# A first stage of attention and MLP laid out as one list of pieces, with one unit's raw tensors kept in half of W2's place

## The chip, the cores and the metric

The kernel runs on one core of a Trainium2 chip. Its engines are PE (TensorE, matmuls), ACT (ScalarE), DVE (VectorE), POOL (GpSimd) and SP (SyncE, which here only issues DMAs). Each engine works through its own instructions in the order of the program and waits on semaphores for the others. The metric is the device time of one execution in microseconds (us); lower is better.

## The reference

Eight batches, twelve heads, 448 tokens, head width 64; then a layer norm and a two-layer MLP of width 768 and 3072 over the heads put side by side.

```python
q_n, k_n = (rmsnorm(q, g_q), rmsnorm(k, g_k))
scores = scale * np.matmul(q_n, k_n.transpose(0, 1, 3, 2))
attn = np.exp(scores - np.max(scores, axis=-1, keepdims=True))
attn = attn / (np.sum(attn, axis=-1, keepdims=True) + 1e-09)
x = np.matmul(attn, v)            # heads side by side: [B, S, 768]
xn = (x - mu) / np.sqrt(var + 1e-06) * g_ln
out = x + np.maximum(xn @ w_ch1, 0.0) @ w_ch2
```

## The kernel before

Heads are worked in pairs (six a batch, 48 in all), and pairs are loaded and normalised in units: units 0 to 3 are batch 0 (1, 1, 2 and 2 pairs), from unit 4 on every unit is two pairs, so units 4, 5 and 6 are batch 1, units 7, 8 and 9 batch 2. A unit's raw q, k and v lie in fp32 in a ring of two tiles (`p_in`, tag `qkv`). The first batch's raw v and q take these two tiles too, its keys lie in hT's place.

The preparation of a unit from 4 on is a dozen pieces named by a letter: b sets up, a squares the keys and c the queries (ACT), d and e sum the squares (DVE), g takes the root (ACT), i multiplies the keys by the gains (POOL), j rounds them to fp16 and k takes what is left over (DVE), l scales the queries and m doubles them, z copies the values (POOL). Then K and Q turn keys and queries on PE, C and D copy them out of PSUM (DVE). S is a score block on PE, E its exponential on ACT, V the product with the values on PE, O the evacuation with the division (DVE), T the statistics (DVE). In batch 0 the same letters serve with the pair or query part behind them (qa, qG, qt, qg, ql, qm, Q, QC are a query part's square, gain, sum, root, scale, doubling, turn and copy).

Batch 0 is treated apart: its three blocks of 128 queries (phases 0, 1, 2) are worked one behind the other, so that the MLP's first layer can begin on block t while the next block's attention runs. A, N and X are aggregation, norm and transpose of a block; U{t}.{k} is a sixth of the first layer for block t (24 matmuls of 128 columns), R{t}.{k} its relu. The second layer runs in four chunks of six matmuls for each block and half of the 768 columns.

The order up to the start of batch 1's attention is written out in `ORDER` and emitted for all five engines exactly so. It ends with the scores of pair 6 and the last block's norm; it holds U0.0 to U1.5, the preparation of unit 4 and the loads L4, L5 and L6. What follows comes from two merged lists: `mlp_chunks(0)` (U2.0 to U2.5, then the 24 down chunks, the left half of the columns first) and the attention steps (seven a pair), which `run_rest` lays between the chunks in proportion, leaving the last TAIL0 = 8 chunks behind the attention. `EARLY` places the pieces of units 5 to 9 among these steps, and a load of unit u + 2 follows unit u's pieces. Batch 1's norm follows the last attention step, its transposes are DMAs on SP's queue, and then batch 1's MLP begins (L878, psH). The later batches go the same way.

Queues: SP issues the loads of units up to 10 (each tensor is one main transfer and two small ones), gln, the DMA transposes and the stores; POOL issues the weights, W1 in three thirds (W0, W1, W2 in the list) and W2 in two halves by columns (W3, W4), at their place among its own instructions.

Some names and lines: U is L641 and R L646; S L585 (batch 0) and L333 (later), E L596 and L351, V L617 and L384 to L386; j and k of batch 0 L466 to L471; a and c L207, d and e L210, i L218, k L229, l L71, z L270 to L276; down chunk L894 and its sum L898; xnT's DMA L860; loads L125 and L133; W1 L785, W2 L790.

Of the kernel before, what the change touches and what calls it, by code (L numbers as in the profile page):

```python
# [27 lines left out]
POOL_HI, POOL_DUP = (0, 1, 2, 4, 5), (4,)  # L28
KN_POOL, COPY_ACT, DUP_POOL = (1,), ('C4', 'QC2.4'), ('2.0', '0.2')
# [3 lines left out]
spread a0 qa0.0 d0 a1 qG0.0 qt0.0 h0 d1 qg0.0 n0 h1 ql0.0 j0 qm0.0 n1 Q0.0 k0 QC0.0 K0 j1 C0  # L33
qa0.2 k1 S0.0.0 a2 S0.0.1 qG0.2 qt0.2 K1 C1 E0.0.0 G W0 d2 qg0.2 S0.1.0 a3 z0 ql0.2 h2 d3
E0.0.1 qm0.2 E0.1.0 S0.1.1 n2 z2 V0.0 Q0.2 h3 qa2.0 QC0.2 j2 n3 E0.1.1 W1 qa1.0 V0.1 k2 j3 z3
qt1.0 K2 C2 qg1.0 qG1.0 L4 k3 K3 S0.2.0 S0.2.1 E0.2.0 C3 E0.2.1 qG2.0 ql1.0 K4 V0.2 C4 S0.3.0
O0.0 S0.3.1 E0.3.1 K5 qm1.0 W2 T0.0 Q1.0 E0.3.0 C5 S0.4.0 G2 Q1.3 E0.4.0 QC1.0 S0.4.1 V0.3
E0.4.1 QC1.3 S0.5.0 E0.5.0 S0.5.1 qt2.0 V0.4 E0.5.1 S1.0.0 E1.0.0 V0.5 S1.0.1 O0.1 E1.0.1
S1.1.0 E1.1.0 S1.1.1 T0.1 V1.0 A0 E1.1.1 S1.2.0 N0 E1.2.0 S1.2.1 V1.1 X0 E1.2.1 S1.3.0 XC0
qg2.0 V1.2 S1.3.1 O1.0 E1.3.0 U0.0 E1.3.1 ql2.0 qa2.4 V1.3 T1.0 S1.4.0 qm2.0 R0.0 S1.4.1 qt2.4  # L40
U0.1 E1.4.1 qG2.4 qg2.4 Q2.0 E1.4.0 ql2.4 Q2.2 R0.1 V1.4 QC2.0 L5 S1.5.0 S1.5.1 QC2.2 E1.5.0
U0.2 qm2.4 E1.5.1 V1.5 R0.2 S2.0.0 O1.1 Q2.4 E2.0.0 S2.0.1 U0.3 T1.1 QC2.4 A1 N1 E2.0.1 S2.0.2
X1 R0.3 W3 S2.1.0 XC1 E2.1.0 U0.4 E2.0.2 S2.1.1 R0.4 U0.5 E2.1.1 S2.1.2 R0.5 S2.2.0 V2.0 E2.2.0
U1.0 b4 a4 E2.1.2 d4 i4 S2.2.1 U1.1 E2.2.1 R1.0 S2.2.2 R1.1 V2.1 W4 E2.2.2 S2.3.0 U1.2 c4 z4
# [31 lines left out]
class _Shared:  # L76
    pass


class _Fast:  # L80


    def __init__(self, ctx, tc, sh, q, k, v, gs, g_ln, w1, w2, out):
# [36 lines left out]
        self.late, self.preps, self.n_scores = [], {}, 0  # L120
# [62 lines left out]
    def pieces(self, u):  # L183
# [9 lines left out]
        def begin():  # L193
            c["t"] = self.loads.pop(u)
            c["ssq"] = self.p_n.tile([128, 2, 14], FP32, tag="ssq", name="ssq", bufs=4)[:, :, 0:g]
            c["rt"] = self.p_n.tile([128, 2, 14], FP32, tag="rt", name="rt", bufs=4)[:, :, 0:g]
            c["rb"] = self.p_n.tile([128, 2, 14], FP32, tag="rq", name="rr_all", bufs=6)[:, :, 0:g]
            c["r", 0], c["r", 1] = c["rb"][:, 0], c["rb"][:, 1]
            c["qn"] = self.p_n.tile([128, 14, 2, D], FP16, tag="qn", name="qn")[:, 0:g]
            c["khl"] = self.p_n.tile([128, 14, 2, D], FP16, tag="khl", name="khl")[:, 0:g]  # L200
            self.units[u] = (c["qn"], c["khl"], m, c["r", 1])

        def square(n):
# [3 lines left out]
            nc.scalar.activation(c["sq", n], c["t"][n], AFT.Square)  # L207
# [9 lines left out]
        def kg():  # L217
            nc.gpsimd.tensor_tensor(  # L218
                out=c["t"][1], in0=c["t"][1],
                in1=sh.gprod.unsqueeze(1).broadcast_to([128, g, D]), op=ALU.mult)  # L220

        def khi():
            if u in POOL_HI:
                nc.gpsimd.tensor_copy(out=c["khl"][:, :, 0], in_=c["t"][1])
            else:
                nc.scalar.activation(c["khl"][:, :, 0], c["t"][1], AFT.Identity)  # L226

        def klo():
            nc.vector.tensor_tensor(out=c["khl"][:, :, 1], in0=c["t"][1],  # L229
                                    in1=c["khl"][:, :, 0], op=ALU.subtract)  # L230

        def qn():
            if u < DMA_UNIT:
                _scaled(nc, c["qn"][:, :, 0], c["t"][0], c["r", 0])
                return
            x, r = c["t"][0], c["r", 0]
# [28 lines left out]
        def qdup():  # L265
            (nc.gpsimd if u in POOL_DUP else nc.vector).tensor_copy(out=c["qn"][:, :, 1],
                                                            in_=c["qn"][:, :, 0])

        def vmain():
            nc.gpsimd.tensor_copy(out=v16.rearrange("p s h j d -> p (s h) j d")[:, :, :, 0:D],  # L270
                                  in_=c["t"][2][:, 0:6 * m].rearrange("p (h j) d -> p h j d", j=3))

        def vleft():
            for e in range(2):
                r = slice(64 * e, 64 * e + 64)
                nc.gpsimd.tensor_copy(out=vl[r, :, e, 0:D], in_=c["t"][2][r, 6 * m:])  # L276
# [42 lines left out]
    def scores(self, p, i):  # L319

        nc = self.nc
        c = self.prs[p]
        u, w = PAIR_UNIT[p]
        both = u >= TWO_LEFT and i == 6
# [3 lines left out]
        if both and w:  # L328
            return
        ps = [self.score_bank(p + d) for d in range(2 if both else 1)]  # L330
        if i < 6:
# [13 lines left out]
        for d, x in enumerate(ps):  # L345
            if i < 6 or (p + d) % 2 == 0:
                o = c["E"][:, i]
            else:
                o = self.prs[p + d]["EL"] = self.p_e.tile([128, S], FP16, tag="EL", name="EL")
            g = self.group(p + d, i)  # L350
            nc.scalar.activation(out=o, in_=x[:, 0:S], func=AFT.Exp,  # L351
                                 scale=self.units[u][3][:, g:g + 1], bias=EXP_BIAS)

        if i == 6 and UNIT_PAIR[u] == p and u > 4:
# [13 lines left out]
    def values(self, p, i):  # L368
        nc = self.nc
# [17 lines left out]
        if i == 6:  # L387
            self.evac_o(p)
# [27 lines left out]
    def first_pieces(self):  # L416
# [34 lines left out]
        def key_unit(u, p0, m):  # L451
# [3 lines left out]
            def square():  # L455
                start(c, g, "khl")
                nc.scalar.activation(c["sq"], k, AFT.Square)

            def scale():
                eng = nc.gpsimd if u in KN_POOL else nc.vector  # L460
                eng.tensor_tensor(out=k, in0=k, in1=c["r"].unsqueeze(2).broadcast_to([128, g, D]),
                                  op=ALU.mult)

            def high():
                if u in POOL_HI:
                    nc.gpsimd.tensor_copy(out=c["n"][:, :, 0], in_=k)  # L466
                else:
                    nc.scalar.activation(c["n"][:, :, 0], k, AFT.Identity)
# [17 lines left out]
        def query_part(ph, p0, p1):  # L486
# [15 lines left out]
            def weight():  # L502
                for y in src:
                    nc.gpsimd.tensor_tensor(
# [11 lines left out]
            def double():  # L516
                eng = nc.gpsimd if tag in DUP_POOL else nc.vector
                eng.tensor_copy(out=c["n"][:, :, 1], in_=c["n"][:, :, 0])
# [33 lines left out]
        def values(z):  # L552
            p0, p1 = {0: (0, 2), 2: (2, 4), 3: (4, 6)}[z]
            nc.gpsimd.tensor_copy(
                out=self.v16[:, p0:p1, :, :, 0:D].rearrange("p s h j d -> p s (h j) d"),
                in_=tv[:, 6 * p0:6 * p1].rearrange("p (s g) d -> p s g d", g=6))
            for e in range(2):
                r = slice(64 * e, 64 * e + 64)
                nc.gpsimd.tensor_copy(out=self.vl[r, p0:p1, e, 0:D], in_=tv[r, 36 + p0:36 + p1])
# [85 lines left out]
        def relu(t, k):  # L645
            nc.scalar.activation(  # L646
                out=self.hT[:, 4 * k:4 * k + 4, ts(t, 128)],
                in_=o["up", t, k].rearrange("p (f s) -> p f s", f=4), func=AFT.Relu)
# [21 lines left out]
    def moved(self, name, out, ps):  # L670
        if name in COPY_ACT:
# [16 lines left out]
    def first_attention(self):  # L688
# [5 lines left out]
        ops = self.ops = self.first_pieces()  # L694
        for x in ORDER:
            key, n = x[0], x[1:]
            if x in ops:
                ops[x]()
            elif x == "batch1":
                self.batch(1)  # L700
            elif x == "spread":
                self.spread_g()
            elif key == "L":
                self.load_unit(int(n))
            elif x == "G":
# [481 lines left out]
```

## Time and profile before

| | us |
|---|---|
| three runs | 620.84, 623.96, 624.11; median 623.96 |
| the profiled execution | 621.17 |
| its span, first to last instruction | 619.5 |
| PE / DVE / ACT / POOL busy over the span | 580.2 / 296.5 / 356.5 / 190.6 |
| first matmul of batch 1's MLP | 139.36 |

A page of a profile shows one execution. Its rows of 40 digits are the busy share of each fortieth of the span in tenths; PEclk is the granted TensorE clock in the same way. Rows of windows give the busy time of each engine in a stretch, with the number of instructions, then the granted clock, the share of DMA time and the rate. Rows of groups name line, engine, operation, output and input, shapes and count, then busy time and the mean in ns of one, then the idle time ahead of them and what ended it. Rows of a timeline or of the chain give start and duration.

### The profile page before, as it was taken

The page shows a single profiled execution, that of the slowest core. Times are in us where ns is not written, and L with a number is a line of the kernel's source. Part 1 is how long each engine was busy: PE and PEld are TensorE (multiplying, and loading weights), DVE is VectorE, ACT ScalarE, POOL GpSimd, SP SyncE. Part 2 cuts the span into 40 slices and gives each one's busy share as a digit, 9 for nine tenths or more (in the row PEclk, how much of TensorE's full clock was granted, in tenths as well). Part 3 has the DMA queues.
Part 4 walks back from the last instruction along what each step waited for, and adds up shares of the span by engine and source line. Part 5 has one row for each costly group of instructions (what it writes and reads, how often), then busy time and mean ns, then how long its engine had stood idle before and what let it go on. Part 6 is the DMA issues. An engine that isn't in the chain of part 4 may idle for free.

```text
span 619.5 us, 12191 instructions
## 1 busy us (share of the span) xinstructions
PE 580.2 (94%) x4856; PEld 358.7 (58%) x4856; DVE 296.5 (48%) x634; ACT 356.5 (58%) x675; POOL 190.6 (31%) x250
## 2 busy tenths in 40 slices
PE   2499869979999999999999999999999999999997
PEld 1489756545456566655456566655556666654465
DVE  5974777772444535671453535662453531360011
ACT  4577767736875189726875189727875187214300
POOL 5843152233445055603535065503522000000000
PEclk9999989999999999999999999999999999999999
DMA  8999963358398468796367489666453420040011
GB/s 253 214 238 215 217 148 100 104 121 229 62 122 157 121 137 124 129 187 136 61 115 170 107 88 209 138 150 119 95 91 86 111 62 4 26 102 2 1 51 54
DMA packets 130224, 75.23 MB, mean 121 GB/s; under 512 B 96468, under 2 KB 120356, under 8 KB 130164
## 3 DMA queue, kind: packets, MB, share of 16 engines
q1 hardware_dynamic: 113092, 44.53, 36.9%
q0 software_dynamic: 16128, 29.27, 22.4%
q8 instruction: 39, 0.64, 0.4%
q10 hardware_dynamic: 944, 0.62, 0.4%
q14 instruction: 21, 0.17, 0.1%
HBM read 52.30 MB, written 11.01 MB: 102 GB/s over the span
## 4 chain that ended last, share of the span: by engine, by line
PE 83%; DVE 8%; ACT 2%; DMA 2%; issue 2%; POOL 1%; SPq 0%; DVEq 0%; ACTq 0%; POOLq 0%
PE psC L894 32%; PE psH L878 31%; PE psS L333 7%; PE oA L384 4%; PE psU L641 3%; PE oB L386 2%; PE psS L339 1%; DVE ssq L210 1%; ACT khl L207 1%; DMA xnT<-xn 1%; DVE xn L832 1%; DVE qn L71 1%; PE psS L585 1%; DVE khl L471 1%; DMA qkv<-in_v_dram 1%
## 5 line engine op out<-in xcount | busy, mean ns | idle before, releaser
L894 PE MATMUL psC<-w,hT 128*128 128x384 f16 (+1 forms) x1368 | 235.6, 323 | 0.0
L878 PE MATMUL psH<-xnT,w 128*128 128x512 f16 (+1 forms) x1008 | 218.4, 356 | 3.0 <-DMA xnT<-xn 3.0
L351 ACT ACTIVATE E<-psS,rr_all 128x448 f16<-128x448 f32 x273 | 170.9, 636 | 54.3 <-PE psS L333 52.6
L894 PEld LDWEIGHTS <-hT 128*128 128x128 f16 x1368 | 126.9, 98 | 79.6 <-issue 5.9
L880 ACT ACTIVATE hT<-psH 128x512 f16<-128x512 f32 (+1 forms) x168 | 93.7, 558 | 121.9 <-PE psH L878 120.3
L878 PEld LDWEIGHTS <-w 128*128 128x128 f16 x1008 | 90.7, 98 | 79.2 <-issue 5.5
L333 PE MATMUL psS<-qU,kU 128*128 128x448 f16 x252 | 87.6, 353 | 8.7 <-ACT E L351 8.1
L384 PEld LDWEIGHTS <-E 128*128 128x128 f16 x819 | 57.2, 98 | 44.4 <-issue 6.2
L218 POOL TENSOR_TENSOR qkv<-qkv,gprod 128x896 f32<-128x896 f32 x21 | 44.3, 2111 | 111.6 <-ACT khl L207 61.5
L898 DVE SCALAR_TENSOR_TENSOR x<-psC,rs_all,x 128x384 f32<-128x384 f32 x48 | 29.3, 616 | 76.1 <-PE psC L894 75.7
L384 PE MATMUL oA<-v,E 128*128 128x65 f16 x756 | 59.4, 194 | 0.4 <-DVE x L401 0.3
L125 POOL DMA_DIRECT2D qkv<-in_k_dram x14 | 11.2, 799 | 134.3 <-ACT E L351 64.3
L399 DVE RECIPROCAL rec_all<-oA 128x6 f32<-128x6 f32 x42 | 8.2, 195 | 91.1 <-PE oA L384 90.8
L210 DVE TENSOR_REDUCE ssq<-khl 128x14 f32<-128x896 f32 x21 | 22.8, 1084 | 51.0 <-ACT khl L207 51.0
L386 PE MATMUL oB<-v,E 128*128 128x65 f16 x252 | 45.8, 194 | 0.2
L71 DVE SCALAR_TENSOR_TENSOR qn<-qkv,rr_all 128x256 f16<-128x256 f32 (+1 forms) x72 | 28.2, 450 | 18.1 <-ACT rr_all L214 17.6
L333 PEld LDWEIGHTS <-kU 128*128 128x128 f16 x252 | 24.7, 98 | 19.8 <-issue 2.2
L210 DVE TENSOR_REDUCE ssq<-qn 128x14 f32<-128x896 f32 x21 | 22.8, 1084 | 24.4 <-ACT qn L207 24.3
L641 PE MATMUL psU<-xnT,w 128*128 128x128 f16 x432 | 27.8, 223 | 0.3 <-DVE xnT L674 0.3
L229 DVE TENSOR_TENSOR khl<-qkv,khl 128x896 f16<-128x896 f32 x21 | 23.2, 1106 | 8.7 <-ACT khl L226 6.4
L386 PEld LDWEIGHTS <-E 128*128 128x128 f16 x273 | 26.4, 97 | 0.6 <-DVE xl L406 0.5
L641 PEld LDWEIGHTS <-w 128*128 128x128 f16 x432 | 26.1, 100 | 0.8 <-issue 0.5
(143 smaller groups left out, 590.5 us busy)
## 6 DMA issues: line engine op xcount, KB each, us to landing
out_dram<-x SPq DMA_DIRECT2D x20, 384.0 KB, 2.6
qkv<-in_v_dram POOLq DMA_DIRECT2D x15, 384.0 KB, 6.2
qkv<-in_k_dram POOLq DMA_DIRECT2D x14, 384.0 KB, 3.8
qkv<-in_q_dram POOLq DMA_DIRECT2D x14, 384.0 KB, 5.3
w<-in_moe_w_ch_dram POOLq DMA_DIRECT2D x3, 1536.0 KB, 13.5
w<-in_moe_w_ch_dram POOLq DMA_DIRECT2D x2, 2304.0 KB, 23.3
qkv<-in_q_dram SPq DMA_DIRECT2D x8, 384.0 KB, 4.8
qkv<-in_v_dram SPq DMA_DIRECT2D x7, 384.0 KB, 12.8
```

The lines of the kernel that those rows point to most:

```text
L71: nc.vector.scalar_tensor_tensor(out=out, in0=x, scalar=8.0, in1=r.unsqueeze(2).broadcast_to([x.shape[0], g, D]), op0=ALU.mult, op1=ALU.mult)
L210: nc.vector.tensor_reduce(out=c["ssq"][:, n], in_=c["sq", n], axis=AX.X, op=ALU.add)
L218: nc.gpsimd.tensor_tensor(out=c["t"][1], in0=c["t"][1], in1=sh.gprod.unsqueeze(1).broadcast_to([128, g, D]), op=ALU.mult)
L333: nc.tensor.matmul(ps[0][:, 0:S], c["main"][:, ts(i, 128)], c["q"][:, ts(h, S)], start=True, stop=True)
L351: nc.scalar.activation(out=o, in_=x[:, 0:S], func=AFT.Exp, scale=self.units[u][3][:, g:g + 1], bias=EXP_BIAS)
L384: nc.tensor.matmul(oA[:, t, cs], E[:, ts(t, 128)], rhs, start=(i == 0 and t == 0), stop=(i == 6 and t == 2))
L386: nc.tensor.matmul(oB[:, cs], E[:, 320:448], rhs, start=(i == 0), stop=(i == 6))
L641: nc.tensor.matmul(ps[:, ts(f, 128)], sh.w1[:, dc, ts(4 * k + f, 128)], self.xnT[:, dc, ts(t, 128)], start=(f == 0 and dc == 0), stop=(f = ...
L878: nc.tensor.matmul(ps[:, 0:N], sh.w1[:, dc, ts(f, 128)], xnT[:, dc, 0:N], start=(dc == 0), stop=(dc == NDC - 1))
L880: nc.scalar.activation(out=hT[:, f, 0:N], in_=ps[:, 0:N], func=AFT.Relu)
L894: nc.tensor.matmul(ps[:, 0:g[1]], hT[:, f, ts(t, 128)], sh.w2[:, f, cols], start=(f == 0), stop=(f == NFF - 1))
L898: nc.vector.scalar_tensor_tensor(out=x[:, cols], in0=ps[:, 0:g[1]], scalar=self.rs[:, b, t:t + 1], in1=x[:, cols], op0=ALU.mult, op1=ALU.add)
```

## The change

`ORDER` now reaches from the first instruction to the end of the first batch's MLP. It holds, beside what it held, all of batch 1's attention (S6.0 to V11.6, with score, exponential and value as pieces of their own), the preparation of units 4 to 8, every U and R, the down chunks as H{t}.{g}.{k} with their sums J and stores P, batch 1's norm as Y.A, Y.N, Y.X and Y.R, and the loads by tensor: L5k, L5q and L5v are unit 5's keys, queries and values. `run_rest` starts at batch 1; pair 12's scores, until now laid ahead of batch 1's MLP, follow its start.

Unit 5 no longer takes a tile of the ring: its raw tensors lie in the place of W2's second half until they are read, and W4 is loaded after that. W2 lies by halves in memory. `ENGINE` says for single pieces which engine does them (A ACT, V DVE, P POOL); what is not named keeps the usual one, and j without an entry goes to ACT.

```diff
-POOL_HI, POOL_DUP = (0, 1, 2, 4, 5), (4,)
-KN_POOL, COPY_ACT, DUP_POOL = (1,), ('C4', 'QC2.4'), ('2.0', '0.2')
+ENGINE = dict(x.split(":") for x in """ C3:A qm0.0:P QC0.0:A QC0.2:A qG2.0:V QC2.2:A qG2.4:V
+qm2.4:P R0.4:V R0.5:V R1.4:V R1.5:V XC2:A R2.0:V R2.1:V R2.2:V R2.3:V a4:V j4:P a5:P c5:P c6:P
+a7:P i7:V j7:P m7:P a8:V j8:P m8:P""".split())
 ORDER = """
...
+spread qa0.0 a0 qt0.0 a1 d0 h0 qG0.0 d1 n0 h1 j0 n1 k0 qg0.0 ql0.0 qm0.0 j1 k1 K0 a2 C0 G W0
+Q0.0 d2 qa0.2 QC0.0 qt0.2 h2 qg0.2 qG0.2 qa1.0 n2 S0.0.0 S0.0.1 ql0.2 K1 L5k C1 qm0.2 E0.0.0 z0
+S0.1.0 j2 qt1.0 a3 Q0.2 k2 qG1.0 E0.0.1 qg1.0 L5q S0.1.1 QC0.2 d3 V0.0 K2 C2 E0.1.1 h3 K3 qa2.0
+E0.1.0 S0.2.0 n3 S0.2.1 V0.1 ql1.0 j3 qm1.0 C3 Q1.0 Q1.3 E0.2.0 k3 qa2.4 W1 K4 z2 qt2.0 S0.3.0
...
+E1.0.0 S1.1.0 E1.0.1 Q2.0 ql2.4 S1.1.1 L5v E1.1.0 L4k E1.1.1 L6k S1.2.0 Q2.2 S1.2.1 T0.0 E1.2.0
+V0.5 S1.3.0 O0.1 E1.2.1 V1.0 T0.1 E1.3.0 S1.3.1 V1.1 S1.4.0 E1.3.1 L4v V1.2 S1.4.1 QC2.0 A0 G2
+E1.4.0 qm2.4 V1.3 S1.5.0 E1.4.1 Q2.4 L4q N0 S1.5.1 E1.5.0 W3 E1.5.1 O1.0 S2.0.0 V1.4 S2.0.1
+E2.0.0 X0 E2.0.1 XC0 V1.5 S2.0.2 b4 a4 QC2.2 S2.1.0 L6q E2.1.0 U0.0 b5 a5 S2.1.1 O1.1 E2.1.1
+E2.0.2 R0.0 T1.1 W2 U0.1 S2.1.2 T1.0 A1 E2.1.2 U0.2 QC2.4 S2.2.0 R0.1 c4 S2.2.1 V2.0 E2.2.1
+E2.2.0 N1 V2.1 X1 S2.2.2 d4 e4 XC1 S2.3.0 L6v U0.3 E2.2.2 E2.3.0 g4 i4 j4 S2.3.1 S2.3.2 E2.3.1
+R0.3 k4 R0.2 d5 K7 E2.3.2 C7 U1.0 S2.4.0 S2.4.1 E2.4.0 K6 S2.4.2 E2.4.1 V2.2 c5 E2.4.2 l4
+S2.5.0 E2.5.0 S2.5.1 m4 V2.3 i5 S2.5.2 E2.5.1 C6 Q6 V2.4 E2.5.2 O2.0 D6 V2.5 R1.0 Q7 O2.1 S6.0
+S6.1 j5 E6.0 U1.1 S6.2 e5 k5 E6.1 S6.3 T2.1 T2.0 z4 b6 a6 U1.2 E6.2 E6.3 L7k S6.4 g5 A2 S6.5
...
+L7v R2.0 U2.1 V7.2 l6 z5 C9 S8.3 k6 V7.3 S8.4 V7.4 Q9 E8.3 V7.5 S8.5 E8.4 E8.5 V7.6 b7 a7 U2.2
+c7 D9 R2.1 O7 S8.6 K10 E8.6 R2.2 V8.0 E9.6 W4 R1.5 U2.3 i7 S9.0 S9.1 U0.5 C10 V8.1 E9.1 V8.2
+L8k d7 E9.0 z7 U2.4 S9.2 R0.5 R2.3 V8.3 S9.3 E9.2 U2.5 e7 S9.4 g7 H0.0.0 l7 V8.4 m6 L8q V8.5
...
+V11.5 i8 C12 V11.6 O11 T11 L9v H0.1.0 H0.1.1 H0.1.2 Y.A Y.N0 j8 g8 Y.R Y.X0 H0.1.3 Q12 Y.N1
+H1.1.0 H1.1.1 Y.X1 Y.N2 J2.0 Y.N3 Y.X2 H1.1.2 Y.X3 H1.1.3 l8 J0.1 k8 m8 J1.1 D12 P0.1 y8 H2.1.0
+z8 L10k H2.1.1 H2.1.2 P2.0 H2.1.3 L10q L10v J2.1 P2.1 P1.1 x8 M
 """.split()
+IN_W2 = 5
-EARLY = {5: (42, 49), 6: (47, 56), 7: (61, 69), 8: (75, 83), 9: (89, 97)}
+EARLY = {9: (89, 97)}
-TAIL0 = 8
...
+    def load_part(self, u, n):
+        b, hs, m = UNITS[u]
+        if u not in self.loads:
+            if u == IN_W2:
+                t = self.sh.w2[:, 1].rearrange("p f d -> p (f d)").bitcast(FP32)[:, 0:42 * D].rearrange(
+                    "p (n g d) -> p n g d", n=3, g=14)
+            else:
+                t = self.p_in.tile([128, 3, 14, D], FP32, tag="qkv", name="qkv")
+            self.loads[u] = [t[:, n] for n in range(3)]
...
         def relu(t, k):
-            nc.scalar.activation(
-                out=self.hT[:, 4 * k:4 * k + 4, ts(t, 128)],
-                in_=o["up", t, k].rearrange("p (f s) -> p f s", f=4), func=AFT.Relu)
+            if ENGINE.get(f"R{t}.{k}", "A") == "A":
+                nc.scalar.activation(out=out, in_=ps, func=AFT.Relu)
+            else:
+                nc.vector.tensor_scalar(out=out, in0=ps, scalar1=0.0, scalar2=None, op0=ALU.max)
...
     def load_w2(self, g):
         self.nc.gpsimd.dma_start(
-            out=self.sh.w2[:, :, ts(g, 384)],
+            out=self.sh.w2[:, g],
...
     def run_rest(self):
-        for b in range(B):
+        for b in range(1, B):
...
-    sh.w2 = const.tile([128, NFF, DM], FP16, name="w2")
+    sh.w2 = const.tile([128, 2, NFF, DM // 2], FP16, name="w2")
```

More of the change, by code (lines that the diff above doesn't have):

```diff
@@ L327, in scores @@
             c["E"] = self.p_e.tile([128, k, S], FP16, tag=f"E{k}", name="E")
[L328 to L329 removed]
         ps = [self.score_bank(p + d) for d in range(2 if both else 1)]
+        for d, x in enumerate(ps):
+            self.prs[p + d]["ps", i] = x
         if i < 6:
```

279 lines of the change are left out of this document (159 added, 120 removed).

## The prediction

> **What bounds the kernel now.** I read the page first, then what TensorE (PE) waited for, then the windows by stage, and groups, chain, timelines and queues only for the first stage.
>
> ```profile
> PE   2499869979999999999999999999999999999997
> PEclk9999989999999999999999999999999999999999
> ```
> ```profile
> PE psH L878 <- DMA xnT<-xn: 3.0, 1, 3.0
> PE psS L333 <- ACT E L351: 0.4, 2, 0.2
> ```
> ```profile
> core 0: us, PE busy (x) PEld busy (x) DVE busy (x) ACT busy (x) POOL busy (x), PEclk, DMA share, GB/s
> 6.14:27.59 21.45, 9.54 (x79) 7.65 (x80) 18.40 (x23) 11.06 (x28) 15.95 (x19) 1.00 1.06 251
> 27.59:68.40 40.81, 38.19 (x658) 36.23 (x657) 27.02 (x49) 30.11 (x62) 16.67 (x16) 1.00 1.19 224
> 68.40:92.34 23.94, 16.58 (x217) 13.48 (x216) 17.96 (x28) 16.84 (x33) 9.46 (x9) 0.93 0.84 171
> 92.34:128.41 36.07, 32.48 (x345) 21.60 (x341) 26.26 (x56) 25.60 (x45) 7.50 (x9) 1.00 0.38 100
> 128.41:139.36 10.95, 7.97 (x50) 4.63 (x49) 8.84 (x18) 2.30 (x5) 4.08 (x5) 1.00 0.63 144
> 139.36:619.50 480.14, 475.41 (x3520) 275.05 (x3520) 196.18 (x452) 269.07 (x502) 134.80 (x186) 1.00 0.53 105
> 0.00:139.36 139.36, 104.75 (x1336) 83.60 (x1337) 100.34 (x182) 87.39 (x173) 55.83 (x64) 0.99 0.83 179
> 139.36:216.46 77.10, 76.97 (x553) 42.71 (x554) 33.50 (x74) 46.91 (x84) 28.17 (x39) 1.00 0.74 139
> ```
>
> The first fence is two rows of the page's 40 slices: PE is full from about the tenth on. The second holds every wait of PE from its first matmul of batch 1's MLP (L878, at 139.36 us) to the end: one of 3.0 us before that matmul, 0.4 after it. From there PE works 475.41 of 480.14 us, and a change of the first stage can win nothing. Ahead of it 104.75 of 139.36 us are busy; 34.6 stand idle, and that is all there is to win.
>
> The windows cut this stretch at the third pair's first exponential (27.59), batch 1's first exponential (68.40), the first down projection (92.34), the last score of batch 1 (128.41) and the start of its MLP. I call them A (up to 27.59), B, C (two rows) and D. In A the full engine is VectorE (DVE), 18.40 of 21.45 us. In B it is PE, 38.19 of 40.81, a share of 94%, DVE and ScalarE (ACT) at two thirds. In C, PE has 69% and then 90%. D ends in the 3.0 us of waiting for xnT.
>
> **A: pieces change engines.** The list puts the high halves j0, j1 and j2 on ACT; they were on GpSimd (POOL).
>
> ```profile
> 20.86 1.83 POOL khl L466
> 22.72 1.78 DVE khl L471
> ```
> ```profile
> 26.09 2.51 DVE L471 TENSOR_TENSOR khl<-hT,khl 128x896 f16<-128x896 f32 x1
> 79.76 2.78 POOL L218 TENSOR_TENSOR qkv<-qkv,gprod 128x896 f32<-128x896 f32 x1
> 80.52 2.97 DVE L71 SCALAR_TENSOR_TENSOR qn<-qkv,rr_all 128x896 f16<-128x896 f32 x1
> 87.67 1.08 DVE L71 SCALAR_TENSOR_TENSOR qn<-qkv,rr_all 128x896 f16<-128x896 f32 x1
> 97.20 1.08 DVE L210 TENSOR_REDUCE ssq<-khl 128x14 f32<-128x896 f32 x1 [0.37 <-ACT khl L207]
> 97.30 2.08 POOL L218 TENSOR_TENSOR qkv<-qkv,gprod 128x896 f32<-128x896 f32 x1 [11.68 <-DMA qkv<-in_v_dram]
> ```
> ```profile
> L468 ACT ACTIVATE khl<-hT 128x896 f16<-128x896 f32 x1 | 0.9, 949 | 0.1
> ```
>
> The chain into 27.59 runs through j2 on POOL (1.83), k2 (1.78) and k3 (2.51) on DVE. On ACT a j of this size took 0.949, so j2 gains 0.9. The k's are long because POOL works beside them: of two equal DVE instructions of L71 the one that began inside a POOL multiplication took 2.97 and ended 0.95 after it, the one beside an idle POOL 1.08; while the reduction at 97.20, with one input, kept its 1.08 under the same POOL line. At 1.08, k2 gains 0.7 and k3 1.4. Sum 3.0, so A ends at 24.6. One end is 6 (DVE's 3.05 us of idle in the window go too). The other is a loss: unit 5's loads now come right behind the first batch's, and their three main transfers of 384 KB (row below) at the window's 251 GB/s are 4.7 us if all went ahead. They stand behind the first loads on SP's queue and only the first W1 third is issued earlier than it was, so I allow a loss of 2.
>
> **B: attention of the first batch with less MLP in it.**
>
> ```profile
> 58.62 1.34 PE psU L641 x24
> 88.23 2.37 PE psU L641 x24
> 93.85 0.34 PE tr L293 x6
> 94.18 0.19 PE psS L333
> 107.57 0.97 PE psC L894 x6
> ```
> ```profile
> L351 ACT ACTIVATE E<-psS,rr_all 128x448 f16<-128x448 f32 x46 | 27.9, 629 | 12.4 <-PE psS L333 11.3 <-PE psS L344 0.8
> L646 ACT ACTIVATE hT<-psU 128x512 f16<-128x512 f32 x18 | 10.7, 594 | 6.7 <-PE psU L641 6.5
> L207 ACT ACTIVATE khl<-qkv 128x896 f32<-128x896 f32 x6 | 5.7, 942 | 0.0
> L229 DVE TENSOR_TENSOR khl<-qkv,khl 128x896 f16<-128x896 f32 x5 | 6.0, 1199 | 2.3 <-POOL khl L224 2.3
> L898 DVE SCALAR_TENSOR_TENSOR x<-psC,rs_all,x 128x384 f32<-128x384 f32 x6 | 3.7, 614 | 1.9 <-PE psC L894 1.8
> ```
>
> Before the last exponential of batch 0 the old list has twelve U, the new one five (U0.0 to U0.3, U1.0). Seven times 1.34 us, 9.4, leave PE in B: 38.19 becomes 28.8. ACT loses their relus (7 x 0.594) and the square a4 (0.942): 30.11 becomes 25.0. DVE gains a4, nearest to the 1.199 of L229, also two reads of 896: 27.02 becomes 28.2. The other swaps (C, QC, qm, qG) exchange pieces of under 1.5 us among engines that here have room; I put them at nothing, covered by the some 12 us that DVE and ACT each have idle in B, and at up to 2 us on DVE if that cover is gone. At the old share of 94%, B lasts 28.8 / 0.94 = 30.8.
>
> One wait is new: c4 on ACT, the square of unit 4's queries, needs a load that was first on SP's queue behind the first batch and is now behind L6k, which cannot start until ql2.4 has read the last raw query.
>
> ```profile
> 25.79 0.37 SPq L125 DMA_DIRECT2D qkv<-in_k_dram  x1
> 34.52 7.69 SPq L133 DMA_DIRECT2D qkv<-in_v_dram  x2
> 43.51 0.37 SPq L125 DMA_DIRECT2D qkv<-in_k_dram  x1
> 49.16 2.09 SPq L133 DMA_DIRECT2D qkv<-in_v_dram  x2
> ```
> ```profile
> qkv<-in_q_dram SPq DMA_DIRECT2D x8, 384.0 KB, 4.8
> ```
> ```profile
> DMA to landing us min/median/max: 12.9/15.4/25.2
> ```
>
> These are the first and last issues of unit 4 and of unit 5: 16.4 and 7.7 us for nine transfers (three main, six small); the last row but one is the queries' time from issue to landing. L6k stands after 16 of the first batch's 42 exponentials, c4 after 30, and four lie in A. At even pace SP goes on at 24.6 + 12/38 x 30.8 = 34.3; L6k, L4v and L4q are nine transfers, so 34.3 + 7.7 + 4.8 = 46.8, and ACT comes to c4 at 24.6 + 26/38 x 30.8 = 45.7. That is 1.1 us of stall; with 16.4 for the issues, 9.8. Behind c4 on ACT stand the last twelve exponentials, and PE's scores wait for those. I take 3, near the lower end, since W3 was in flight under the 7.7 as it will be here. B lasts 33.8 and ends at 58.4.
>
> **C and D.** PE had 16.58 + 32.48 = 49.06 in C and 7.97 in D, 57.0. To it come the 9.4 from B. The U that ran at a low clock (2.37 for 1.34; the window's clock is 0.93) gives back 1.0. Pair 12 leaves: its scores, pair 13's last block and the turns K13 and Q13 are no longer ahead of batch 1's MLP: some 8 x 0.19 and two turns of 0.40 (the 0.34 above and its first matmul) plus the wider last blocks, 2.7. Makes 62.7. DVE had 17.96 + 26.26 + 8.84 = 53.1; eight relus come (0.6 each, by the 0.614 of L898, also out of PSUM), a8 and i7 (1.2 each), and the 1.9 of the long L71 may go: 58.4. I take PE's share from the second row of C, 90%, since what stood idle in the first is now fed by U's and H's between the scores: 62.7 / 0.9 = 69.7. DVE would then be 84% busy, which is why I take no better share. Ends: 95% (66.0), and 82% as over all of C (76.5).
>
> In D the list lays 12 down chunks (0.97 each) behind the last attention piece, over aggregation, norm and xnT transposes; it was 8. 11.7 us against the old 10.95: of the 3.0 us of waiting I leave 0.5.
>
> W2's second half (W4) goes behind unit 5's last read and behind a7 on POOL, and I cost it at nothing. The W loads took 12.9 to 25.2 us to land. Between W4 and the first H that reads it the list has 4 U, 12 H, 19 scores and 4 turns, 5.4 + 11.6 + 3.6 + 1.6 = 22.2 us of PE beside the values. At 25.2 some 3 us would show. W3 before H0.0.0 and the last W1 third before U0.4 have more.
>
> **Sum.** 24.6 + 33.8 + 69.7 + 0.5 = 128.6 against 139.36: 10.8 won. Pair 12's 2.7 come back in batch 1's MLP, which has PE full (76.97 of 77.10); its seven exponentials (4.4 us) fit ACT's 46.91 there. Net 8.1. The profiled execution took 621.17 us (span 619.5 and 1.7 around it), so 613.1. The median of the runs is 623.96, 2.8 above that execution; by it, 615.9. I predict 614.5, between the two. This likeliest case alone spans 609 to 621: A at its best and 2 us less stall, or the stall of 9.8.
>
> **Rivals.**
>
> *It packs better* (606): A gains 6, no stall at c4, C at 95%: 21.6 + 30.8 + 66.0 + 0.5 = 118.9 would even give 603; half-way is 606. For it: 34.6 us idle. Against: DVE would stand at 90% through C and no row shows a stretch in which PE and DVE were both that full.
>
> *DVE stands behind POOL* (621): after 27.59 POOL gets squares (a5, c5, c6, a7) beside the multiplications i4, i5, i6 and i8: eight pieces of 2.1 us and more that read SBUF twice, where six were. Each that meets a two-input piece of DVE (k, l) costs up to 1.9 (2.97 less 1.08). Four meetings are 7.6, with DVE then the bound: 613.1 + 7.6 = 620.7, no gain to speak of against runs of 621 to 624. Against: of the old six only one met so after 68.40.
> The Trainium skill, "SBUF — State Buffer", section "Who interferes with whom", has one rule for this: an exclusive lock on the port pair that VectorE and GpSimd share, whole instructions long. By that rule the 2.97 is no accident, and the trace agrees (0.95 us after POOL's end); were all eight to meet, by the rule 15 us, against one in six by the rows, 2.5.
>
> *Unit 4's queries come late* (630, slower): if ql2.4 is not earlier than it was, SP goes on at 43.5; nine issues at unit 4's old pace, 16.4, and 4.8 to land make 64.7 for c4. Twelve of 38 exponentials are left, 9.9 us: batch 1 then begins at 74.6 and not at 68.4, with seven U more to do: 74.6 + 69.7 + 0.5 + 1.0 of cold clock = 145.8, so 6.4 + 2.7 slower, 630. It decides against the change once the queries land 8.1 us later than the 48.7 that my 3 us of stall mean, from 57 on. For it: unit 4's row. Against: unit 5's 7.7 under a load of W in flight.
>
> **How the numbers follow.** Forecast 0.50, packs better 0.20, DVE behind POOL 0.14, late queries 0.16. The range 604 to 627 leaves out most of the last and the best part of the second, some 0.2. A difference of 0.5% (3.1 us from 623.96) is about what a measurement of this kernel tells from none: faster is under 620.8, slower over 627.1. Faster takes the forecast, the second and a part of the third: 0.72; same 0.13; slower 0.15.
>
> **What would show it.** A: k2 and k3 near 1.1 us, third pair's first exponential near 24.6. B: ACT's wait for in_q at c4, 3 us or ten; batch 1's first exponential near 58. C: PE's share 90%, no U at 2.4 us, DVE pieces of k and l at 1.1 or near 3. D: first L878 at about 128.6, its wait under 1 us. A PE wait for w at the second down half would add what I left out; a first L878 later than 137 proves the forecast wrong.

## The result and the profile after

The changed kernel takes 616.07 us (median of four runs, 613.76 to 618.04) against 623.86 in the same set of runs: a ratio of 0.989, interval 0.985 to 0.993. The profiled execution took 615.57 us, its span 613.9, 5.6 less than the 619.5 of before. Ratios and intervals, here and below, leave out runs in a slow state (one of "unit 5 last", one of "+ W2 and W0"), medians don't.

PE and PEclk are again the rows of the page's 40 slices:

```profile
PE   2494999999999999999999999999999999999997
PEclk9998999999999999999999999999999999999999
```

The hole now lies in the fourth slice (46 to 61 us), where it wasn't, and from the fifth on PE is full. The windows by stage are cut at the third pair's first exponential (E0.2.0, 30.18), batch 1's first exponential (70.12) and the first matmul of batch 1's MLP (130.62). The fourth row is D alone (it runs 0.16 us into the MLP), the last two are the rest in two pieces:

```profile
core 0: us, PE busy (x) PEld busy (x) DVE busy (x) ACT busy (x) POOL busy (x), PEclk, DMA share, GB/s
6.11:30.18 24.07, 10.10 (x87) 8.68 (x88) 17.52 (x24) 14.65 (x34) 13.02 (x15) 1.00 1.09 255
30.18:70.12 39.94, 29.95 (x484) 27.60 (x482) 27.72 (x52) 25.25 (x55) 14.78 (x12) 0.91 1.11 222
70.12:130.62 60.50, 59.81 (x748) 45.63 (x747) 53.43 (x102) 33.13 (x64) 21.32 (x21) 1.00 0.60 125
...
118.69:130.78 12.09, 12.09 (x80) 7.43 (x79) 11.57 (x25) 0.42 (x2) 3.09 (x4) 1.00 0.47 108
...
130.62:210.87 80.25, 79.84 (x577) 44.08 (x576) 37.64 (x81) 52.84 (x94) 32.43 (x45) 1.00 0.79 149
210.87:613.90 403.03, 398.61 (x2970) 232.47 (x2967) 162.80 (x378) 222.49 (x418) 106.63 (x147) 1.00 0.49 98
```

A ended 5.6 us later than forecast (30.18 for 24.6), B lasted 6.1 longer (39.94 for 33.8), and C with D was 9.7 shorter (60.50 for 70.2). So batch 1's MLP began at 130.62, 2.0 us from the forecast 128.6, by errors that cancel. In C and D, PE worked 59.81 of 60.50 us.

Where A and B lost it, ACT's timeline says; the number in brackets is the idle time ahead of the instruction and what ended it. The first row is the square of the last block's first queries, which came in batch 0's own load; the second is E0.1.0, held up behind it; the third is c4:

```profile
27.70 0.42 ACT L549 ACTIVATE qn<-qkv 128x256 f32<-128x256 f32 x1 [5.97 <-DMA qkv<-in_q_dram]
28.02 0.58 ACT L645 ACTIVATE E<-psS 128x512 f16<-128x512 f32 x1
...
57.78 0.95 ACT L111 ACTIVATE qn<-qkv 128x896 f32<-128x896 f32 x1 [9.10 <-DMA qkv<-in_q_dram]
```

Both waits are in the chain that ended last, as transfers of 14.59 and 12.25 us:

```profile
13.02 14.59 DMA qkv<-in_q_dram
41.48 2.52 SPq L169
45.43 12.25 DMA qkv<-in_q_dram
60.29 2.51 PE psU L690 x24
```

The first was issued from 10.27 on. The second was issued from 44.04 on, behind unit 5's loads (in SP's timeline those with w, since they lie in W2's place) and behind L4k, L6k and L4v:

```profile
10.27 3.41 SPq L169 DMA_DIRECT2D qkv<-in_q_dram  x2
13.72 0.61 SPq L803 DMA_DIRECT2D gln<-in_moe_g_ln_dram  x1
14.38 0.51 SPq L161 DMA_DIRECT2D w<-in_k_dram  x1
14.94 6.05 SPq L169 DMA_DIRECT2D w<-in_k_dram  x2
21.03 0.60 SPq L161 DMA_DIRECT2D w<-in_q_dram  x1
21.67 9.67 SPq L169 DMA_DIRECT2D w<-in_q_dram  x2
...
36.18 0.52 SPq L161 DMA_DIRECT2D qkv<-in_k_dram  x1
...
44.04 0.69 SPq L161 DMA_DIRECT2D qkv<-in_q_dram  x1
44.77 2.54 SPq L169 DMA_DIRECT2D qkv<-in_q_dram  x2
```

PE pays for c4 with 8.47 us of waiting until an exponential frees the scores' place, and right after that wait a U takes 2.71 us, where later ones take 1.34 (the window's granted clock is 0.91):

```profile
59.22 0.32 PE L634 MATMUL psS<-qU,kT 128*128 128x192 f16 x1 [8.47 <-ACT E L645]
...
60.08 2.71 PE L690 MATMUL psU<-xnT,w 128*128 128x128 f16 x24
```

### The profile page after: what moved, and what is told of

Its sections match the earlier page's. It is cut to its first block, busy times and chain, and to the rows that moved or that the text cites. A ratio compares the mean times of both kernels' runs of the same rounds, so it can differ in the third digit from the quotient of the medians.

```text
span 613.9 us, 12177 instructions
## 1 busy us (share of the span) xinstructions
PE 578.3 (94%) x4856; PEld 358.5 (58%) x4856; DVE 301.0 (49%) x646; ACT 350.3 (57%) x666; POOL 190.4 (31%) x247
## 4 chain that ended last, share of the span: by engine, by line
PE 88%; DMA 5%; SPq 2%; DVE 2%; ACT 2%; issue 1%; ACTq 0%; DVEq 0%
PE psC L1004 35%; PE psH L970 31%; PE psS L381 8%; PE oA L439 5%; DMA qkv<-in_q_dram 4%; PE psU L690 3%; PE oB L441 2%; SPq L169 1%; PE psS L387 1%; SPq L161 1%; DMA hT<-in_k_dram 1%; PE tr L332 0%; ACT E L402 0%; PE psS L634 0%; PE tr L349 0%
## 5 line engine op out<-in xcount | busy, mean ns | idle before, releaser
L261 POOL TENSOR_TENSOR qkv<-qkv,gprod 128x896 f32<-128x896 f32 x19 | 40.3, 2120 | 87.6 <-ACT khl L111 33.3
L86 DVE SCALAR_TENSOR_TENSOR qn<-qkv,rr_all 128x256 f16<-128x256 f32 (+2 forms) x71 | 26.5, 433 | 17.5 <-ACT rr_all L257 17.5
L634 PE MATMUL psS<-qU,kT 128*128 128x128 f16 (+2 forms) x76 | 10.1, 254 | 17.7 <-ACT E L645 14.5
```

Of the source, the lines that this page charges most:

```text
L86: nc.vector.scalar_tensor_tensor(out=out, in0=x, scalar=8.0, in1=r.unsqueeze(2).broadcast_to([x.shape[0], g, D]), op0=ALU.mult, op1=ALU.mult)
L261: _on(nc, f"i{u}", "P").tensor_tensor(out=self.loads[u][1], in0=self.loads[u][1], in1=sh.gprod.unsqueeze(1).broadcast_to([128, g, D]), op= ...
```

## The experiments

Each kernel was timed beside the kernel before on its chip; ratios are to that. In the experiments line numbers are one below those of the changed kernel, three where the engine table shrank. The diffs are cuts from the list and show where a load is put, not always where it is taken from. Three slips in the expectations: the one for unit 5's loads calls "the third pair's first exponential" what is E0.1.0, the second pair's last (28.02 in the changed kernel); the last one writes E2.0.0 for E0.2.0; and W0 to W3 are issued by POOL, not SP. Stage ends below are E0.2.0, batch 1's first exponential and the first psH of batch 1's MLP, from each profiled execution, with the largest waits for transfers in it (first queries and c4: ACT; U: PE, at a sixth of the first layer; a5 and z4: POOL, at squares of unit 5 and copies of unit 4; a6: ACT, at squares of unit 6).

| kernel | median | ratio (interval) | A ends | B ends | MLP | waits for transfers |
|---|---|---|---|---|---|---|
| before | 623.86 | 1 | 27.59 | 68.40 | 139.36 | xnT 3.0 |
| changed | 616.07 | 0.989 (0.985, 0.993) | 30.18 | 70.12 | 130.62 | first queries 6.0, c4 9.1 |
| unit 4 first | 613.33 | 0.988 (0.985, 0.991) | 27.77 | 59.02 | 125.92 | first queries 3.5, U 3.7 |
| queries of 4 ahead | 610.56 | 0.983 (0.979, 0.986) | 27.84 | 58.20 | 125.24 | first queries 3.7, c4 0.3, U 4.9 |
| W0 later | 615.81 | 0.991 (0.987, 0.994) | 25.46 | 69.97 | 130.47 | c4 12.1 |
| unit 5 last | 622.16 | 1.000 (0.997, 1.003) | 28.01 | 76.07 | 136.57 | first queries 3.7, c4 8.3, a5 20.8 |
| + W2 ahead of W3 | 605.66 | 0.976 (0.972, 0.979) | 29.03 | 59.71 | 120.20 | first queries 4.7, c4 1.5 |
| + W2 and W0 | 611.17 | 0.978 (0.970, 0.985) | 25.40 | 65.50 | 126.00 | c4 8.1, z4 6.1 |
| old engines | 613.81 | 0.987 (0.984, 0.990) | 27.05 | 61.39 | 128.86 | U 5.8 |
| relus on ACT | 611.54 | 0.984 (0.981, 0.987) | 24.96 | 59.84 | 119.60 | c4 3.4 |
| ring | 614.00 | 0.988 (0.984, 0.993) | 27.67 | 59.53 | 128.64 | first queries 3.4, a6 6.2 |
| unit 4 first, W | 611.50 | 0.985 (0.980, 0.989) | 25.49 | 65.82 | 126.23 | a5 13.8 |
| between | 606.09 | 0.976 (0.970, 0.981) | 25.59 | 56.37 | 119.39 | z4 9.2 |
| values too | 606.78 | 0.979 (0.975, 0.983) | 25.38 | 56.16 | 121.02 | a6 3.3 |

### Which load stands ahead of which

**Unit 4's three loads ahead of unit 5's.**

```diff
-S0.0.1 ql0.2 K1 L5k C1 qm0.2
+S0.0.1 ql0.2 K1 L4k L4q L4v L5k L5q L5v C1 qm0.2
```

> The only edit is the order of loads on SP: unit 4's keys, queries and values stand where unit 5's keys stood, unit 5's follow, unit 6's keys stay last. In the changed kernel ACT waits 6.0 us for the first batch's small query transfers (to 27.7) and 9.1 us for unit 4's queries (to 57.8). Theory SP (unit 5's nine transfers, issued from 14.4 to 36.1, stand in front of everything): SP now stops until z3 has read the first values, some 23 us, so both waits go; batch 1's first exponential falls from 70.1 to about 58 and the time by 8 to 10 us, to 607. Theory W (the weights, issued 2.5 to 4 us earlier than before, take the DMA engines): the first wait stays near 6, the queries still need some 12 us to land but start before 30, so only the second wait goes: 611.

**Only L4q, from behind Q2.4 to right behind L4k.**

```diff
-S1.1.1 L5v E1.1.0 L4k E1.1.1 L6k
+S1.1.1 L5v E1.1.0 L4k L4q E1.1.1 L6k
...
-E1.4.1 Q2.4 L4q N0
+E1.4.1 Q2.4 N0
```

> The only edit: unit 4's queries go right behind unit 4's keys, ahead of unit 6's keys and unit 4's values. Their main issue moves from 44.0 to about 38.5 us. If the second wait is the place in SP's queue alone, it falls from 9.1 by the 5.5 us to about 3.6 and the time by 4 to 5, to 611.5. If it is the DMA engines' load (W3 issued at 39.1, W2 at 42.2), the queries land hardly earlier and the time stays within 2 us of 616. The first wait stays at 6 in both.

In both, c4's wait goes (0.34 us at 46.84 in the second) and batch 1's attention begins at 59.02 and 58.20; the forecast had 58.4. Moved ahead of two other loads in SP's queue, L4q alone makes B 30.36 us long in place of 39.94, and with the 2.3 us by which A ended earlier, batch 1's attention begins 11.9 us earlier. The first wait stays, at 3.5 and 3.7 us for 6.0; the second edit changes nothing ahead of it, so A's 2.3 us are not its doing. And a wait that the changed kernel doesn't have appears at the first U of the last W1 third; its load, W2, is issued behind W3. ACT's two squares and PE, in the kernel with L4q ahead:

```profile
25.36 0.42 ACT L548 ACTIVATE qn<-qkv 128x256 f32<-128x256 f32 x1 [3.65 <-DMA qkv<-in_q_dram]
...
46.84 0.95 ACT L110 ACTIVATE qn<-qkv 128x896 f32<-128x896 f32 x1 [0.34 <-DMA qkv<-in_q_dram]
```
```profile
69.46 2.58 PE L689 MATMUL psU<-xnT,w 128*128 128x128 f16 x24 [4.85 <-DMA w<-in_moe_w_ch_dram]
```

So of the 11.9 us won at batch 1's first exponential, 5.4 are left at batch 1's MLP (125.24 for 130.62). By their times the first kernel can't be told from the changed one (0.988 for 0.989), and it won less than either theory expected (607 and 611); the second is about what its first theory expected (611.5), though c4's wait fell further than to 3.6.

**W0 alone later**, behind z0 (about 17 us, where it was issued at 11.39).

```diff
-a2 C0 G W0 Q0.0
+a2 C0 G Q0.0
...
-E0.0.0 z0 S0.1.0
+E0.0.0 z0 W0 S0.1.0
```

> The only edit: the first third of W1 is issued behind z0 on POOL, at about 17 us and not 11.4 (it was 13.9 in the kernel before). Theory W: the first batch's small query transfers, issued until 13.7, land before it and the first wait falls from 6.0 to under 2, batch 1's first exponential comes 4 us earlier. Theory SP: unit 5's keys from 14.4 on are what slows them, the first wait stays above 4 and the time within 2 us of 616.

The first wait goes and A ends 4.7 us earlier, at 25.46; but c4's queries land as before, so its wait grows from 9.10 to 12.10, and B ends at 69.97, where it did. So W0's place makes the first wait: none of the five kernels that issue it behind z0 has it. How long it is with W0 early varies: 6.0 us in the changed kernel, and 3.7, 4.7 and none in three others (queries of 4 ahead, W2 ahead of W3, relus on ACT) whose pieces and loads are the same up to there. Moved alone, W0 wins no time (615.81 for 616.07). The same small transfers, two of 96 KB (groups of DMA issues; the last number is the median us from issue to landing), in the kernel before, the changed one, the one with W0 later, and the one with the relus on ACT:

```profile
qkv<-in_q_dram SPq DMA_DIRECT2D x2, 96.0 KB, 5.9
```
```profile
qkv<-in_q_dram SPq DMA_DIRECT2D x2, 96.0 KB, 13.8
```
```profile
qkv<-in_q_dram SPq DMA_DIRECT2D x2, 96.0 KB, 5.0
```
```profile
qkv<-in_q_dram SPq DMA_DIRECT2D x2, 96.0 KB, 7.3
```

In the changed kernel SP issues them from 10.27 to 13.68, a little earlier than before; what differs is that POOL's W0 goes out at 11.39, in their midst, and before at 13.94, when they were all but issued (rows of POOL's queue, the changed kernel first).

```profile
11.39 0.88 POOL L877 DMA_DIRECT2D w<-in_moe_w_ch_dram  x1
```
```profile
13.94 0.88 POOL L785 DMA_DIRECT2D w<-in_moe_w_ch_dram  x1
```

The Trainium skill, "DMA: Bandwidth & Descriptors", section "Issuing engines are not separate DMA queues", says that what SP, ACT and POOL issue runs on the same 16 DMA engines and interleaves. The traces agree: 5.0 us to land with W0 issued after them, 13.8 with it issued among them; only with the relus on ACT, W0 at 11.76 among them too, they landed in 7.3.

**Unit 5's loads behind L4q**, none of them early.

```diff
-K1 L5k C1
+K1 C1
...
-E1.4.1 Q2.4 L4q N0
+E1.4.1 Q2.4 L4q L5k L5q L5v N0
```

> The only edit: unit 5's loads go behind unit 4's queries; unit 4's keys and unit 6's keys are then the first behind gln. Theory SP: the first wait goes (nothing follows gln until z3 is done), the third pair's first exponential comes at 23 and not 28; unit 4's queries still wait for ql2.4 through unit 6's keys, so the second wait falls to about 4: 608. Theory W: first wait stays at 6, time within 3 us of 616.

Nothing is left of the gain: POOL waits 20.8 us for unit 5's keys at a5, c4 still waits 8.3, batch 1 begins at 76.07. That unit 5's loads are early is needed. That they alone are in c4's way falls with this run, and the first wait neither goes nor stays at 6 but is 3.7: SP came to L6k at 36.31 (it had to wait until the last raw query was read) and to L4q at 41.54, hardly earlier than the 44.04 of the changed kernel. What holds L4q up here is its place behind L6k; c4's square began at 54.21, 12.7 us after the issue began.

**W2 ahead of W3, on top of L4q ahead; then W0 later as well.**

```diff
-E1.5.0 W3 E1.5.1
+E1.5.0 W2 W3 E1.5.1
...
-T1.1 W2 U0.1
+T1.1 U0.1
```

> Based on the experiment that moved only unit 4's queries ahead (610.56, batch 1's first exponential 58.20, first MLP matmul of batch 1 at 125.24, one PE wait of 2.6 to 4.9 us for w near 69 us). Here the last W1 third (W2) is also issued ahead of W3. Theory O (the weight wait is only the order of two loads on SP's queue): the wait for w at the first U of the last third goes, with the U at a low clock behind it, first MLP matmul about 121.5, time 605 to 607. Theory B (the loads of this stretch share one bandwidth, whichever comes first the other is late by as much): the wait moves to W3's first reader or to unit 6, time 609 to 611.

> The same, and W0, the first W1 third, back behind z0 on SP's queue. Theory W (the wait of 3.7 us for the first batch's queries comes from W0 lying ahead of their landing): the wait goes, the third pair's first exponential at 24.6 or earlier, and since nothing downstream is hidden now by a later wait, time 602 to 604. Rival (what ends A is the DVE work, the wait only hides it): A ends no earlier than 25.3 and the time is that of the kernel with W2 ahead of W3, within 1 us; or W1 and W2, pushed back by W0, are late and make a PE wait for w.

The first is as theory O has it: no PE wait for w is left, C and D take 60.5 us (59.71 to 120.20), 605.66 us. With W0 later the first wait goes too, A ends at 25.40, and yet it isn't faster: now c4 waits 8.1 us. SP issued c4's queries there from 26.53 on, earlier than in the first, but the last of them only at 34.85, as W2 and W3 went out (35.00 and 35.90), and it took 17.08 us to land. Its four runs are 603.78, 610.90, 611.45 and 613.99, and the trace is of the 610.90; the one at 603.78 may have landed its loads otherwise, which no trace shows. The windows of A and B shown here have a DMA share of 1.06 to 1.19, before and after: the stretch is full. Of the orders tried here all but the one with W2 ahead of W3 made another load late by bringing one forward.

**All of unit 4 first; unit 5's keys, then unit 4's keys and queries, then unit 5's queries and values ("between"); the same with L4v ahead of L6k.** In all three W2 and W0 stand as in the last.

```diff
-S0.0.1 ql0.2 K1 L5k C1 qm0.2
+S0.0.1 ql0.2 K1 L4k L4q L4v L5k L5q L5v C1 qm0.2
```

> All of unit 4's loads ahead of unit 5's on SP's queue, W0 behind z0 and the last W1 third ahead of W3 on POOL's. Theory O (what is late is what stands behind something not yet needed; the transfers fit once they are in the order of their due times): no wait for queries in A and at c4, none of PE for w; A's third pair begins at 25, batch 1's first exponential at 56 to 57, first MLP matmul of batch 1 at 117, time 600 to 602. Rival (the stretch up to 58 us is full of transfers, so any order leaves one late, as when W0 alone or W0 and W2 were moved): the late one is now unit 5's values or keys, or W0 at U0.0; time 604 to 611.

```diff
-S0.0.1 ql0.2 K1 L5k C1 qm0.2
+S0.0.1 ql0.2 K1 L5k L4k L4q L5q L5v C1 qm0.2
```

> Unit 5's keys first, then unit 4's keys and queries, then unit 5's queries and values, W0 behind z0, the last W1 third ahead of W3. Theory O: no wait over 1 us for queries or for w, time 600 to 603. Rival (the stretch is full): unit 4's values or W0 late, time 604 to 611.

```diff
-E1.1.0 E1.1.1 L6k S1.2.0
+E1.1.0 E1.1.1 L4v L6k S1.2.0
```

> As the kernel with unit 5's queries and values between unit 4's queries and unit 6 (606.09; 604.19 in the profiled execution, with E2.0.0's stage ends at 25.59, 56.37 and 119.39), and unit 4's values ahead of unit 6's keys, since POOL waited 9.2 us for them at 60.42. Theory O: that wait goes, E0.2.0 stays near 25.6 and batch 1's first exponential near 56.4, the first MLP matmul of batch 1 comes at 117 to 118, profiled execution 601 to 603, median 603 to 605. Rival (POOL's wait cost nothing, and the stretch is full): time within 1.5 us of 606, or unit 6's keys late at their squares in place of the values.

The first falls to its rival: unit 5's keys are late by 13.8 us. In the second neither ACT nor PE waits over 0.5 us for queries or W, and its windows are A and B much as the forecast made them without a stall: A ends at 25.59 for 24.6, and B lasts 30.78 us for 30.8 (the third row is C with D):

```profile
6.11:25.59 19.48, 9.69 (x84) 8.22 (x85) 18.07 (x24) 14.64 (x33) 13.51 (x16) 1.00 1.06 266
25.59:56.37 30.78, 29.48 (x487) 27.48 (x486) 28.75 (x52) 25.40 (x56) 14.28 (x9) 1.00 1.15 230
56.37:119.39 63.02, 60.25 (x747) 45.59 (x746) 54.10 (x102) 33.24 (x64) 20.77 (x24) 1.00 0.80 164
```

What is late there are unit 4's values (POOL 9.2 us at z4), and C with D takes 63.0. With the values ahead, unit 6's keys are late instead (3.3 us at a6), C with D takes 64.9, and nothing is won (606.78). The best, 605.66 with W2 ahead of W3 and 606.09 with unit 4 between, beat both kernels and can't be told apart.

### The engines, the relus and the ring

All three start from the kernel with L4q ahead (610.56).

```diff
-ENGINE = dict(x.split(":") for x in """ C3:A qm0.0:P QC0.0:A QC0.2:A qG2.0:V QC2.2:A qG2.4:V
...
+ENGINE = dict(x.split(":") for x in """ j0:P j1:P j2:P j4:P j5:P m4:P n1:P C4:A QC2.4:A qm2.0:P qm0.2:P""".split())
```

> The kernel with unit 4's queries ahead (610.56), but every piece on the engine that it had before the change. Theory E (the engines by piece are worth what I summed: 3 us in A from k2 and k3, and little elsewhere): k2 and k3 are 1.8 and 2.5 us again, A ends 2 to 3 us later, all relus and the squares on ACT in C; time 613 to 615. Rival (the queries' wait of 3.7 us in A hides the k's, and C has room on ACT): time within 1 us of 610.6. Rival (DVE is near its bound in C at 76 to 86 per cent, so taking relus off it gains): 608.

```diff
-qm2.4:P R0.4:V R0.5:V R1.4:V R1.5:V XC2:A R2.0:V R2.1:V R2.2:V R2.3:V a4:V
+qm2.4:P XC2:A a4:V
```

> The kernel with unit 4's queries ahead (610.56), but the eight relus that the change put on DVE back on ACT, 8 x 0.6 = 4.8 us more on ACT in C (33 of 55 us busy) and 5.5 less on DVE (41 of 55). Theory P (PE sets the pace of C, both other engines have room): time within 1 us of 610.6. Rival (ACT's exponentials release the scores in order, so each relu ahead of one delays PE by its 0.6): up to 4.8 us slower, 615.

With the old engines it is 613.81, as theory E had it (though the intervals, 0.987 and 0.983, just overlap), but not where it had it. The windows of A, B, and C with D, then B and C with D of the kernel it starts from:

```profile
6.11:27.05 20.94, 8.94 (x79) 7.52 (x79) 18.09 (x23) 10.50 (x28) 13.86 (x18) 1.00 1.09 269
27.05:61.39 34.34, 30.45 (x494) 27.52 (x492) 26.63 (x48) 27.49 (x58) 16.91 (x18) 1.00 1.07 211
61.39:128.86 67.47, 61.40 (x748) 47.08 (x747) 46.15 (x95) 40.41 (x76) 16.25 (x18) 0.95 0.68 143
```
```profile
27.84:58.20 30.36, 29.05 (x484) 26.88 (x482) 28.59 (x52) 25.30 (x55) 15.71 (x12) 1.00 1.16 228
58.20:125.24 67.04, 61.50 (x747) 47.19 (x746) 53.07 (x102) 33.41 (x64) 19.78 (x21) 0.97 0.71 148
```

A ends at 27.05, with 0.5 us of the first wait; with the new engines and none of that wait, six kernels of the table have 24.96 to 25.59. So in A the engines are worth 1 to 2 us and not 3.0. B lasts 34.34, where the same list with the new engines has 30.36: 4.0 us, in swaps that the prediction put at nothing, or at 2; which of them costs it no run here separates. C with D is 67.47 for 67.04, with a wait of 5.8 for W in it in place of 4.9. The relus on ACT cost nothing that can be measured (0.984 for 0.983). The profiled execution was its fastest run, 604.27, in which neither the first queries nor W2 made anyone wait; no stage of it should be read as the relus' doing.

**Unit 5 back in the ring**, its loads behind unit 4's, unit 6's behind z4, unit 7's behind z5.

```diff
-IN_W2 = 5
+IN_W2 = -1
...
-E1.3.1 L4v V1.2
+E1.3.1 L4v L5k L5q L5v V1.2
...
-T2.0 z4 b6
+T2.0 z4 L6k L6q L6v b6
```

> The kernel with unit 4's queries ahead (610.56, batch 1's first exponential at 58.20), but unit 5 back in the ring of two tiles: its loads follow unit 4's, unit 6's follow z4 and unit 7's follow z5. Theory B (W2's half as a third place is what lets units 5 and 6 be there in time): unit 6, now behind z4 at about 60 us, lands some 15 us later and batch 1's scores of its pairs wait for it; time 616 to 622, no faster than before. Rival (the list alone makes the gain, the ring would do): time within 2 us of 610.6, since without unit 5's nine early transfers the first wait for queries (3.7 us) goes too.

614.00: slower than with W2's half (0.988 for 0.983; the intervals just overlap), by less than I expected, and faster than before. Unit 6's keys are late (6.2 us on ACT, 5.8 on PE), so C with D takes 69.1 us. My theory had the direction and the place, not the size; the rival that the ring would do as well (within 2 us) falls narrowly. With the list as it is, half of W2 as a third place is worth some 3.5 us (614.00 less 610.56).

## Why the prediction was right

The total came out within 1.6 us of the forecast, the direction too. That so near a hit came of these steps is luck: A and B lost 11.7 us on the forecast, C and D won 9.7, each for reasons of its own.

- **A** was forecast to end at 24.6 and ended at 30.18. The failed step is "only the first W1 third is issued earlier than it was, so I allow a loss of 2": it was the right load, but I kept it as a bound of 2 and out of the sum, where it was 6.0 us of waiting (and W1's second third was issued earlier too, at 18.72 for 22.64); and I had not seen that the square which waits stands ahead of the scores' next exponential on ACT. Where W0 was moved and nothing else, A ended at 25.46. How long the wait is varies, as said, so part of the 6.0 is chance. The gain from k2 and k3 was partly had; on DVE's timeline they took

```profile
17.88 1.83 DVE L520 TENSOR_TENSOR khl<-hT,khl 128x896 f16<-128x896 f32 x1
...
29.47 1.09 DVE L520 TENSOR_TENSOR khl<-hT,khl 128x896 f16<-128x896 f32 x1 [5.26 <-ACT khl L103]
```

where I had 1.08 twice. The 1.83 ends at 19.71, 0.94 after another POOL multiplication (16.92, 1.85 long): taking j2 off POOL did not leave POOL idle beside k2. It is the same lag, 0.95, that the prediction read off one row of before.
- **B**: the working 28.8 / 0.94 = 30.8 stands; 30.78 was measured where no load of B was late, and 30.68, with PE at 28.85, with W2 ahead of W3. The term that failed is c4's stall, "I take 3, near the lower end": it was 9.1, near the upper bound of 9.8 that the prediction gave by unit 4's own pace. Its issues were to end at 42.0 (34.3 and 7.7) and ended at 47.3 (44.77 and 2.54), and the last small transfer took 12.25 us to land, not 4.8. The 4.8 was the median of the main transfers; c4 waits for the small ones behind them too, and those had a median of 9.5 on the same view of before:

```profile
qkv<-in_q_dram SPq DMA_DIRECT2D x14, 32.0 KB, 9.5
```

With 9.5 the working gives 42.0 + 9.5 = 51.5 and a stall of 5.8.
- **C and D**: 70.2 was forecast and 60.50 came. Two terms were off: PE's work, too large (62.7 for 59.81; 0.6 of that left with pair 12, the rest is open), and the share, too low at 90%, which was 59.81 / 60.50 = 99%. My reason not to take more, that no row showed PE and DVE both that full, was true of the old list and says nothing of the new one: DVE is at 53.43 of 60.50, 88%. The old engines give the same 67 us in C and D as the new ones, with a like wait for W in both, and outside that wait PE stood idle for under 1 us in either (67.47 less 61.40 and 5.8; 67.04 less 61.50 and 4.9). So it is the order of the list and not the engines that fills PE. This is the rival "it packs better", right in C and D, even beyond its 66.0, and hidden in the total by A and B.
- **D** has no wait: its 12.09 us are all PE work, and the xnT wait of 3.0 is gone. **W4** cost nothing, as forecast. **Pair 12** came back as 3.3 us in batch 1's MLP (80.25 for 76.94), against 2.7; all that follows it is equal (403.03 and 403.20).
- **The rivals**: DVE behind POOL: k's and l's were held up three times in C and D, taking 1.52, 2.29 and 1.57 us, some 2 us more than alone together, each ending 0.94 or 0.95 us after a POOL instruction beside it. Only one of the three met a piece that the rival named (a7), the others met copies, and PE was full beside them. Unit 4's queries were late, and landed at 57.7, past the point (57) from which I had it decide against the change; but not by the steps named there. SP went on at 38.48 and not at 43.5, and the nine issues took 8.8 us and not 16.4; it was the landing that took longer. It didn't decide, since C and D gave 9.7 us more than I had allowed for. With C and D as I had them, 70.12 + 70.2 = 140.3 and pair 12's 2.7 would have made the span some 4 us longer: the rival's sign, if not its size.

## What to carry to other kernels

When a list moves loads, go through the queues in order of due times and ask, for each consumer on ACT or PE, which transfers of all queues are in flight ahead of its load; where the DMA share is already over 1, as in A and B here, take the landing time of the slowest like transfers (here the small ones), not the median of the large ones. A stall removed in such a stretch mostly returned at the next late load here: judge an order by the first matmul after the full stretch, not by the wait that went. A busy share read from the old order is no upper bound for a list laid by hand: 90% became 99%.

## What the runs showed of the hardware

- SP's time to issue is no constant. Two transfers of 32 KB took it 9.67 us at 21.67 in the changed kernel and 6.05 at 14.94 (rows above). In the kernel with W0 alone later, the same two pairs of unit 5's keys and queries took 1.26 and 1.25 (SP's timeline):

```profile
15.33 1.26 SPq L168 DMA_DIRECT2D w<-in_k_dram  x2
17.27 1.25 SPq L168 DMA_DIRECT2D w<-in_q_dram  x2
```

So a queue that lands late also issues late, and every load behind it moves. The only edit between the two is W0's place; whether W0's own transfer sets the 9.67, or SP's earlier transfers that it holds up, no run here separates.

- Kernels whose pieces and loads are the same up to there landed the first queries' two small transfers in different times: 13.8 us in the changed one, 11.6 with the queries of unit 4 ahead, 7.3 with the relus on ACT, W0 issued among them each time. Whole times of one kernel differ too: the relus-on-ACT kernel ran at 604.27 once and 609.53 to 611.75 in its other four runs, the one with W2 and W0 moved at 603.78 once, 610.90 and 611.45. That other runs of one kernel land their loads otherwise is likely from this, but only one run of each was traced; a single profile of such a kernel should be read as one of several pictures.
